# Each engine's order of steps, and each tile's buffer, from a written list instead of a planner

## The chip, the cores and the metric

The kernel runs on one core of one Trainium2 chip. The metric is the device time of one execution in microseconds (us). Engines are named as the profile names them: PE is TensorE, PEld its weight loads, DVE is VectorE, ACT is ScalarE, POOL is GpSimd, SP is SyncE.

## What is computed

Causal attention over a window of 96 keys plus 8 global ones, with a distance bias for each head, and then a two-layer MLP with h - tanh(h) between. All inputs and the output are float32.

```python
# q, k, v: (4, 8, 768, 64); w_in: (512, 2048); w_out: (2048, 512)
scores = q @ k.T / sqrt(64) + bias          # bias = -slope[head] * distance
keep = (key < 8) | ((0 <= row - key) & (row - key < 96))
a = softmax(where(keep, scores, -1e9))
x = (a @ v), heads side by side             # (3072, 512)
h = x @ w_in
out = (h - tanh(h)) @ w_out                 # (3072, 512)
```

## The kernel before, in words

The 3072 rows are cut into 24 **units** of 128 rows (4 batches of 6 blocks). The first block of every batch comes first, so units 0 to 3 need one block of keys, and the others two: their own (o=0) and the one before (o=1); a few columns of the batch's first block stand in for the global keys. A step has a name, a unit and perhaps a block, and one engine:

- `lk.u`, `lq.u`, `lv.u`: the loads of k, q and v, cast to bf16 on the way (L390, L393), on POOL's DMA queue; unit 0's k and q come as float32 on SP's and ACT's queues and are cast by `ck.0`, `cq.0`. `in.j`, `out.j` load parts of the weights (L396, L399), also on POOL.
- `rel`, `dist`, `slopes`, `first`, `turn`, `ident`, `ones`: constants, `rel` on POOL (L331), the others on DVE. `bm.m` (PE, L371) and `em.m` (ACT, L376) make three masks.
- `T.u` transposes q and k: on PE for units 0 to 6 (L408, L413, L417), with copies out of PSUM `Te.u.j` (ACT or DVE, L325, L327); from unit 7 on by a DMA on SP's queue (L425).
- `B.u` (units 0 to 2, L371) puts the bias into the scores' banks, `S.n` (L444) computes scores, `E.u.o` (ACT, L451) exponentiates, `M.u.o` (DVE, L455) multiplies the mask from unit 3 on, `AV.u` (PE, L470) multiplies with v, which has a column of ones for the sum, and `R.u` (DVE, L478, L479) divides. `K.u` and `V.u` (DVE) copy the global keys and values.
- `X.u` and `Xe.u` transpose the result: on PE (L490) and a copy for units 0 to 7, by a DMA on SP's queue (L501) from unit 8 on.
- The MLP goes by **groups**: units 0 and 1 alone, then two units each. `m1.g.f` (PE, L512) computes two of 16 column blocks of h (four for a single unit), `th.g.f` is tanh (ACT, L522), `g.g.f` subtracts (DVE, L528), `m2.u.c.a` (PE, L537) adds a quarter of the second product, `ev.u.c` copies the sum to SBUF (ACT or DVE, L325, L327) and `st.u.c` stores it (L546), on POOL for units 0 to 20 and on SP behind that.

All engines work through their own steps in order. The order is drawn up in Python while the program is built. `Plan` (from L17) holds every step with its engine, an estimated duration, its predecessors and what it takes and gives back: PSUM has 8 banks, and there are 5 buffers of `kq`, 12 of `vb`, 11 of `qk`, 5 of `pr`, 3 of `x`, 4 each of `xT`, `th`, `g` and `ot`. `Plan.run` (L59) walks through time and starts on every free engine the ready step with the best priority; loads and DMA transposes finish after an estimated time plus a slack. `AHEAD` and `T_AHEAD` (L557, L561) tie the scores and transposes to the progress of m1, `HOLD` (L560) keeps seven steps back. Where PE would stand still before 6.0 us of planned time, `warm` (L760) puts matmuls on a tile of zeros whose result nobody reads (lines 763 to 770). The buffers that the planner gave out are looked up by `buf`, `bank` and `banks` (L305 to L315). What a step waits for on the chip follows from the tiles that it reads and writes. SP's and POOL's DMAs take turns on 8 semaphores each, and a DMA waits for the one before it on its semaphore.

Of the kernel before, what the change touches and what calls it, by code (L numbers as in the profile page):

```python
# [16 lines left out]
class Plan:  # L17


    LAT = {PE: 0.21, ACT: 0.06, DVE: 0.06, POOL: 0.12, SP: 0.06}  # L20
    SLACK_DMA = 1.5
    SLACK_DT = 3.0
    SHARED = 2.5
    KEEP = 9
    BEHIND = (14.0, 23.5, 33.0)
    SLACK_ENG = 0.2
    EDGES = (20.0, 30.0, 180.0, 190.0)

    def __init__(self):
        self.ops, self.pools, self.paired, self.hold, self.cold = {}, {}, set(), {}, 0.0  # L30

    def pool(self, name, n, late=None):
        self.pools[name] = [0.0] * n
        for i, t in (late or {}).items():
            self.pools[name][i] = t

    def op(self, key, eng, us, fn, after=(), take=(), give=(), pri=0.0, ring=None, work=0.0, lag=0.0, tail=0.0,
           us2=None):
        self.ops[key] = dict(
            key=key, eng=eng if isinstance(eng, tuple) else (eng,), us=us, us2=us2, fn=fn,  # L40
            after=[a for a in after if a is not None], take=list(take), give=list(give), pri=pri, ring=ring,
            total={p: sum(m for _, x, m in take if x == p) for _, p, _ in take},
            work=work, lag=lag, tail=tail, n=len(self.ops),
        )

    def choose(self, p, n, have, now):
        have = sorted(g for g in have if g[0] <= now + 1e-9)
        if len(have) < n:
            return None
        if p not in self.paired:  # L50
            return sorted(i for _, i in have[:n])
        when = {i: t for t, i in have}
        both = sorted((max(when[i], when[i + 1]), i) for i in when if i % 2 == 0 and i + 1 in when)
        if n > 1:
            return sorted(i + j for _, i in both[: n // 2] for j in (0, 1)) if len(both) >= n // 2 else None
        lone = [g for g in have if g[1] ^ 1 not in when]
        return [(lone or have)[0][1]]

    def run(self, free):  # L59
        ops = self.ops  # L60
        need, users = {}, {}
        for key, o in ops.items():
            deps = set()
            for a in o["after"]:
                kind, k = ("issue", a[1]) if a[0] == "issue" else ("done", a)
                if k not in ops:
                    raise KeyError((key, a))
                deps.add((kind, k))
            need[key] = len(deps)
            for d in deps:  # L70
                users.setdefault(d, []).append(key)
        holds, left = {}, {}
        for key, o in ops.items():
            for g in o["give"]:
                left[g] = left.get(g, 0) + 1
        avail = {p: [(t, i) for i, t in enumerate(ts)] for p, ts in self.pools.items()}
        late = sorted({t for ts in self.pools.values() for t in ts if t > 0})
        events, tick = [], 0
        ready = {e: [] for e in (PE, ACT, DVE, POOL, SP)}
        busy = dict(free)  # L80
        order, start = [], {}
        rings, upto, version = {}, 0.0, 0

        def margin(t, most):
            a, b, c, d = self.EDGES
            return most * min(1.0, max(0.0, min((t - a) / (b - a), (d - t) / (d - c))))

        def push(t, what, key):
            nonlocal tick
            tick += 1  # L90
            heapq.heappush(events, (t, tick, what, key))

        def fits(o, now):
            left = {p: avail[p] for p in o["total"]}
            for h, p, n in o["take"]:
                ids = self.choose(p, n, left[p], now)
                if ids is None:
                    return False
                left[p] = [g for g in left[p] if g[1] not in ids]
            return True  # L100

        def drop(kind, key):
            for k in users.get((kind, key), ()):
                need[k] -= 1
                if need[k] == 0:
                    for e in ops[k]["eng"]:
                        ready[e].append(k)

        def flow(now):
            nonlocal upto  # L110
            live = [r for r in rings.values() if r]
            for r in live:
                r[0][1] -= (now - upto) / len(live)
            upto = now

        def again(now):
            nonlocal version
            version += 1
            live = [r for r in rings.values() if r]
            if live:  # L120
                push(now + max(0.0, min(r[0][1] for r in live)) * len(live), "flow", version)

        for e in busy:
            push(busy[e], "free", e)
        for t in late + sorted(self.hold.values()):
            push(t, "free", None)
        for key in ops:
            if need[key] == 0:
                for e in ops[key]["eng"]:
                    ready[e].append(key)  # L130
        while events:
            now, _, what, key = heapq.heappop(events)
            if what == "done":
                for g in ops[key]["give"]:
                    left[g] -= 1
                    if left[g] == 0:
                        h, part = g
                        p, ids = holds[h]
                        for i in ids if part is None else [ids[j] for j in part]:
                            avail[p].append((now, i))  # L140
                drop("done", key)
            elif what == "issued":
                drop("issue", key)
            elif what == "enter":
                flow(now)
                rings.setdefault(ops[key]["ring"], []).append([key, ops[key]["work"]])
                again(now)
            elif what == "flow":
                if key != version:
                    continue  # L150
                flow(now)
                for e, r in rings.items():
                    while r and r[0][1] <= 1e-9:
                        k, _ = r.pop(0)
                        more = margin(now, self.SLACK_DMA) + sum(1.0 for t in self.BEHIND if t < now < 40.0)
                        if k[0] in ("T", "Xe"):
                            shared = any(x for y, x in rings.items() if y is not e)
                            more = margin(now, self.SLACK_DT) + (self.SHARED if shared else 0.0)
                        push(now + ops[k]["tail"] + more, "done", k)
                again(now)  # L160
            if events and events[0][0] <= now + 1e-9:
                continue
            for e in (PE, ACT, DVE, POOL, SP):
                if busy[e] > now + 1e-9:
                    continue
                best, kept = None, False
                for k in sorted(ready[e], key=lambda x: (ops[x]["pri"], ops[x]["n"])):
                    o = ops[k]
                    if self.hold.get(k, 0.0) > now + 1e-9 or kept and "bank" in o["total"]:
                        continue  # L170
                    if fits(o, now):
                        best = ((o["pri"], o["n"]), k)
                        break
                    kept = kept or o["total"].get("bank", 0) >= self.KEEP
                if best is None:
                    continue
                k = best[1]
                o = ops[k]
                for x in o["eng"]:
                    ready[x].remove(k)  # L180
                for h, p, n in o["take"]:
                    ids = self.choose(p, n, avail[p], now)
                    avail[p] = [g for g in avail[p] if g[1] not in ids]
                    holds[h] = (p, ids)
                us = o["us"] if e is o["eng"][0] or o["us2"] is None else o["us2"]
                if e is PE and now < self.cold:
                    us *= 2.0
                end = now + us
                busy[e] = end
# [8 lines left out]
        if len(start) < len(ops):  # L198
            raise RuntimeError(f"no way on: {[k for k in ops if k not in start][:8]}")
# [617 lines left out]
```

## Time and profile before

| what | value |
|---|---|
| three executions | 215.68, 214.89, 214.81 us; median 214.89 us |
| span of the profiled execution, first to last instruction | 213.1 us |
| PE busy, DVE, ACT, POOL | 206.2, 130.8, 116.0, 79.8 us |
| m1 matmuls (L512), m2 matmuls (L537) | 90.2 and 85.7 us busy |
| first filler matmul, first mask matmul | 0.99, 3.10 us |
| first m1 matmul | 18.46 us |
| last PE instruction ends | 210.2 us |
| DMA of POOL's queue, DMA of SP's and ACT's queues | 18.88 MB and 7.61 MB |

The page gives the span of the profiled execution and not its own device time; the three executions lie 1.7 to 2.6 us over that span. Busy times of PE count overlapping matmuls with a modelled end, so two neighbouring steps can seem to overlap by some tenths of a us; distances between starts are exact. 19 of 400 records of L537 are missing from the trace.

### The profile page before, as it was taken

Reading aid. Unit: us, or ns where it says so; the run is one execution under the profiler, and the core shown is the slowest. Engines: PE = TensorE matmul, PEld = TensorE weight load, DVE = VectorE, ACT = ScalarE, POOL = GpSimd, SP = SyncE. Lnnn points to the kernel's source line nnn. Section 1 sums busy time; section 2 is a strip of 40 time slices with the busy share of each in tenths; the row PEclk is TensorE's granted clock in tenths of the full one; section 3 lists DMA queues with packets and bytes.
Section 4 is the critical chain, followed back from the end, with each engine's and each line's share of the span. In section 5 each row is a group of like instructions: output and inputs, shape, how many; then the busy total and the mean of one; then the engine's idle time right before and its main releaser. Section 6 shows DMA issues by size and latency. Waiting matters only on the chain.

```text
span 213.1 us, 5043 instructions
## 1 busy us (share of the span) xinstructions
PE 206.2 (97%) x2053; PEld 142.4 (67%) x2073; DVE 130.8 (61%) x267; ACT 116.0 (54%) x172; POOL 79.8 (37%) x105
## 2 busy tenths in 40 slices
PE   7998999999999999999999999999999999999994
PEld 2567876858656865965965955875855874968643
DVE  6469746727647972883872765891765795754600
ACT  4866535648455562864562753941935763545421
POOL 7995354659577404913603525401011100111000
PEclk9999999999999999999999999999999999999999
DMA  6999999999999993994993998987121411201012
GB/s 132 145 175 201 198 190 198 167 159 215 150 190 162 184 201 99 148 189 112 136 151 67 139 131 128 132 189 113 49 71 55 123 28 25 77 32 67 3 49 100
DMA packets 100886, 27.06 MB, mean 127 GB/s; under 512 B 91840, under 2 KB 99264, under 8 KB 100864
## 3 DMA queue, kind: packets, MB, share of 16 engines
q0 software_dynamic: 73088, 18.88, 92.3%
q1 hardware_dynamic: 27504, 7.61, 22.5%
q8 instruction: 16, 0.26, 0.5%
q10 hardware_dynamic: 272, 0.26, 0.5%
q14 instruction: 6, 0.05, 0.1%
HBM read 27.26 MB, written 6.29 MB: 157 GB/s over the span
## 4 chain that ended last, share of the span: by engine, by line
PE 91%; DVE 3%; DMA 3%; issue 1%; POOL 1%; ACT 0%; POOLq 0%; DVEq 0%
PE ps L512 39%; PE ps L537 39%; PE ps L470 5%; PE ps L444 5%; DMA kq<-in_q_dram 3%; PE ps L417 1%; DVE x L479 1%; PE ps L490 1%; DVE slopes L361 0%; PE ps L408 0%; POOL vb L393 0%; DVE qk L327 0%; POOL kq L390 0%; DVE rden L478 0%; DVE pr L455 0%
## 5 line engine op out<-in xcount | busy, mean ns | idle before, releaser
L512 PE MATMUL ps<-xT,w_in_bf 128*128 128x256 bf16 (+1 forms) x832 | 90.2, 264 | 0.0
L537 PE MATMUL ps<-w_out_bf,g 128*128 128x512 bf16 (+2 forms) x381 | 85.7, 370 | 1.2 <-issue 0.3
L512 PEld LDWEIGHTS <-w_in_bf 128*128 128x128 bf16 x832 | 74.5, 98 | 10.7
L522 ACT ACTIVATE th<-ps 128x512 f32<-128x512 f32 x96 | 56.0, 604 | 32.6 <-PE ps L512 29.3
L528 DVE TENSOR_TENSOR g<-ps,th 128x512 bf16<-128x512 f32 x96 | 62.5, 682 | 12.7 <-ACT th L522 11.8
L537 PEld LDWEIGHTS <-g 128*128 128x128 bf16 x400 | 37.4, 98 | 38.3
L451 ACT ACTIVATE pr<-ps 128x1024 bf16<-128x1024 f32 x44 | 42.5, 1023 | 20.5 <-PE ps L444 20.5
L546 POOL DMA_DIRECT2D out_dram<-ot x21 | 12.1, 574 | 95.1 <-ACT ot L325 71.0
L455 DVE TENSOR_TENSOR pr<-pr,mk 128x1024 bf16<-128x1024 bf16 x41 | 27.8, 688 | 10.9 <-ACT pr L451 10.7
L325 ACT COPY ot<-ps 128x512 f32<-128x512 f32 (+2 forms) x17 | 9.5, 560 | 33.8 <-PE ps L537 33.8
L393 POOL DMA_DIRECT2D vb<-in_v_dram x24 | 21.6, 900 | 6.2 <-DMA w_out_bf<-in_moe_w_out_dram 3.4
L393 POOL DMA_DIRECT2D kq<-in_q_dram x19 | 17.0, 897 | 5.7 <-PE ps L470 2.0
L393 POOL DMA_DIRECT2D kq<-in_k_dram x19 | 17.1, 899 | 3.5 <-DMA qk<-kq 1.6
L479 DVE TENSOR_TENSOR x<-ps,rden 128x512 bf16<-128x512 f32 x24 | 16.6, 692 | 0.8
L327 DVE COPY qk<-qk 128x32 bf16<-128x32 bf16 x16 | 3.6, 228 | 19.3 <-PE ps L444 19.3
L470 PEld LDWEIGHTS <-pr 128*128 128x128 bf16 x352 | 13.4, 97 | 2.8 <-ACT pr L451 0.4
L470 PE MATMUL ps<-vb,pr 128*128 128x65 bf16 x352 | 14.7, 193 | 0.4 <-ACT pr L451 0.2
L444 PEld LDWEIGHTS <-qk 64*128 64x128 bf16 x352 | 10.1, 94 | 7.1 <-issue 6.5
L478 DVE RECIPROCAL rden<-ps 128x8 f32<-128x8 f32 x24 | 5.0, 207 | 15.3 <-PE ps L470 14.9
L444 PE MATMUL ps<-qk 64*128 64x128 bf16 x192 | 9.5, 218 | 0.4 <-DVE rden L478 0.3
L444 PE MATMUL ps<-qk,qk 64*128 64x128 bf16 x160 | 7.8, 216 | 0.0
L327 DVE COPY ot<-ps 128x512 f32<-128x512 f32 x8 | 5.5, 692 | 3.0 <-PE ps L537 2.9
(43 smaller groups left out, 65.3 us busy)
## 6 DMA issues: line engine op xcount, KB each, us to landing
out_dram<-ot POOLq DMA_DIRECT2D x21, 256.0 KB, 3.9
vb<-in_v_dram POOLq DMA_DIRECT2D x24, 128.0 KB, 6.9
kq<-in_k_dram POOLq DMA_DIRECT2D x23, 128.0 KB, 5.9
kq<-in_q_dram POOLq DMA_DIRECT2D x23, 128.0 KB, 6.5
w_out_bf<-in_moe_w_out_dram POOLq DMA_DIRECT2D x4, 512.0 KB, 13.6
w_in_bf<-in_moe_w_in_dram POOLq DMA_DIRECT2D x3, 512.0 KB, 12.1
w_in_bf<-in_moe_w_in_dram POOLq DMA_DIRECT2D x2, 256.0 KB, 6.2
out_dram<-ot SPq DMA_DIRECT2D x2, 256.0 KB, 2.0
```

Of the source, the lines that this page charges most:

```text
L325: nc.scalar.copy(out=out, in_=in_)
L393: eng(e).dma_start(out=dst, in_=rows_of(src, u).rearrange("h p d -> p h d"))
L444: nc.tensor.matmul(bank(("s", u, o), hh)[:, p * P : (p + 1) * P], buf(("qk", back[u] if o else u))[r, 1, p, :], buf(("qk", u))[r, 0, p, :] ...
L451: nc.scalar.activation(d, banks(("s", u, o), 0, 1), AF.Exp, bias=0.0, scale=scale)
L455: nc.vector.tensor_tensor(out=t, in0=t, in1=mk[:, mask_of(u, o)], op=ALU.mult)
L470: nc.tensor.matmul(t[:, h // (H // 2), h % (H // 2), :], buf(("p", u, o))[:, slot(h), :], buf(("v", back[u] if o else u))[:, h, :], start= ...
L479: nc.vector.tensor_tensor(out=buf(("x", u)).rearrange("q (a h) d -> q a h d", a=2), in0=t[:, :, :, 0:Dh], in1=rden.to_broadcast([P, 2, H / ...
L512: nc.tensor.matmul(t[:, (f - f0) * n : (f - f0 + 1) * n], w_in_bf[j][:, c, fo : fo + P], x[:, c, 0:n], start=(c == 0), stop=(c == CD - 1),)
L522: nc.scalar.activation(h_view(buf(("th", g, f0)), g, m), h_view(bank(("h", g, f0)), g, m), AF.Tanh, bias=0.0, scale=1.0)
L528: nc.vector.tensor_tensor(out=buf(("g", g))[:, f0 : f0 + m, 0:n], in0=h_view(bank(("h", g, f0)), g, m), in1=h_view(buf(("th", g, f0)), g, ...
L537: nc.tensor.matmul(bank(part)[:, 0 : c1 - c0], buf(("g", g))[:, f, t * P : (t + 1) * P], w_out_bf[f // FJ][:, f % FJ, c0:c1], start=(f == ...
L546: eng(e).dma_start(out=out[turn_of[u] * P : (turn_of[u] + 1) * P, c0:c1], in_=buf(("ot", u))[:, c0:c1])
```

## The change

The planner is gone, with the durations, priorities and slacks that fed it. The source now holds two lists. `ORDER` names all 792 steps in one row; each engine works through its own in that order. Where a step can run on ACT or DVE, `/a` or `/d` says which. `HOMES` says which buffer or which PSUM banks a tile has. The functions that do the steps are the same, and so are the numbers of buffers. Three things differ in what runs. The word `warm` does not occur in `ORDER`, so there are no matmuls on zeros. 26 steps move between ACT and DVE; ACT has 177 steps (173 before) and DVE 218 (222). The order differs on every engine: PE's differs from its first step (`bm.0 B.0 bm.2 T.0 T.3` now, `bm.1 bm.2 bm.0 B.0 T.0` before), POOL's starts with `lq.3` ahead of `rel`, units 2 and 3 are loaded ahead of unit 1, v of units 0 and 1 is the last v ahead of the first weights, and the sums of several units (`m2`) are open at once.

```diff
-class Plan:
...
-    def run(self, free):
...
-        return order, start, {h: ids for h, (p, ids) in holds.items()}, now
+ORDER = """
+lq.0 lk.0 zero lq.3 ones.0 table rel lk.3 dist lq.2 slopes lk.2 first turn lk.1 bm.0 ident ones.1 lq.1 B.0 cq.0/a
+ck.0/d bm.2 lk.4 em.0 T.0 lv.3 em.2 T.3 lq.4 Te.0.0/d Te.0.1/a lv.2 B.2 Te.3.1/d Te.3.0/a T.2 lv.0 S.3 Te.2.1/a
+Te.2.0/d lv.1 E.3.0 S.2 T.1 in.1 E.2.0 M.3.0 in.0 S.0 Te.1.1/d AV.3 Te.1.0/a in.2 B.1 R.3 E.0.0 S.1 lv.4 AV.2 T.4 R.2
+E.1.0 out.0 AV.0 in.3 Te.4.0/d X.2 Te.4.1/a AV.1 Xe.2/d out.1 X.3 bm.1 R.1 Xe.3/a lq.5 em.1 R.0 S.4 lk.5 E.4.1 K.4 X.0
+X.1 Xe.0/d m1.2.2 Xe.1/d E.4.0 in.4 M.4.1 m1.2.0 th.2.2 M.4.0 m1.1.0 th.2.0 g.2.2 m1.0.0 th.1.0 g.2.0 lv.5 m1.2.4
+g.1.0 th.0.0 out.2 m1.0.4 g.0.0 th.2.4 g.2.4 m1.2.6 th.0.4 m1.1.4 g.0.4 th.2.6 out.3 g.2.6 AV.4 th.1.4 m2.1.0.0 R.4
+m2.2.0.0 V.4 g.1.4 m2.0.0.0 X.4 lq.7 m1.2.8 Xe.4/a m1.2.10 th.2.8 m1.0.8 g.2.8 th.2.10 lk.7 g.2.10 m1.1.8 th.0.8 lk.6
+g.0.8 m2.0.0.1 th.1.8 lq.6 T.5 g.1.8 m2.1.0.1 Te.5.1/a Te.5.0/d S.5 m2.2.0.1 E.5.0 K.5 lk.9 m1.2.12 E.5.1 M.5.0 lv.9
+m1.0.12 th.2.12 M.5.1 m1.1.12 th.0.12 g.2.12 AV.5 th.1.12 g.0.12 m2.3.0.0 V.5 R.5 m1.2.14 lq.9 g.1.12 X.5 th.2.14
+m2.0.0.2 Xe.5/d g.2.14 m1.3.10 lk.8 m1.3.2 th.3.10 lq.8 m1.3.6 g.3.10 th.3.2 lq.13 m1.3.8 g.3.2 T.7 th.3.6 m2.1.0.2
+g.3.6 lv.6 th.3.8 m2.2.0.2 g.3.8 T.9 T.6 m2.3.0.1 lk.10 Te.6.1/a Te.6.0/d m2.1.0.3 lv.7 T.8 S.6 ev.1.0/a m2.2.0.3
+E.6.1 K.6 m1.3.14 ev.2.0/d lq.11 E.6.0 m2.0.0.3 M.6.1 th.3.14 M.6.0 S.7 ev.0.0/a g.3.14 m1.3.4 E.7.1 K.7 m2.3.0.2
+lk.12 th.3.4 M.7.1 m1.3.0 E.7.0 g.3.4 lq.10 AV.6 th.3.0 lk.11 M.7.0 m1.3.12 R.6 lv.8 m2.3.0.3 th.3.12 g.3.0 lq.12 S.9
+ev.3.0/a V.6 m2.4.0.0 g.3.12 lk.14 E.9.1 K.9 AV.7 st.2.0 E.9.0 M.9.1 m2.4.0.1 V.7 m2.5.0.0 T.10 R.7 S.8 M.9.0 T.11 X.6
+E.8.0 m2.4.0.2 Xe.6/d X.7 E.8.1 M.8.0 m2.4.0.3 T.12 Xe.7/d AV.9 ev.4.0/a M.8.1 m2.5.0.1 V.9 R.9 AV.8 lk.15 m1.4.2 R.8
+Xe.9 lv.10 m1.4.14 th.4.2 Xe.8 lk.13 S.10 g.4.2 th.4.14 m1.4.4 lv.12 E.10.0 K.10 g.4.14 m1.4.6 lv.16 th.4.4 M.10.0
+m1.4.8 E.10.1 lk.17 g.4.4 m2.5.0.2 lv.11 th.4.6 M.10.1 m1.4.0 th.4.8 g.4.6 lq.17 g.4.8 S.11 th.4.0 lq.18 m2.5.0.3
+E.11.0 K.11 g.4.0 st.1.0 m1.5.8 E.11.1 M.11.0 m1.4.12 T.13 th.5.8 M.11.1 m1.5.2 th.4.12 g.5.8 m2.6.0.0 th.5.2 g.4.12
...
+g.12.14 m2.21.0.2 m2.20.0.3 m2.22.0.3 ev.20.0/a m2.21.0.3 st.20.0 ev.22.0/a m2.23.0.0 st.22.0 ev.21.0/a st.21.0
+m2.23.384.0 ev.23.0/a st.23.0 ev.23.384/a st.23.384
+"""
+HOMES = """
+mk.0:0,1 mk.1:0,1 mk.2:4,5 f32.0.k:1 kq.0:0 f32.0.q:0 kq.1:3 v.0:2 v.1:3 kq.2:2 kq.3:1 v.2:1 kq.4:4 v.3:0 v.4:4 kq.5:0
+v.5:5 kq.6:2 v.6:7 kq.7:1 v.7:8 kq.8:4 v.8:9 kq.9:3 v.9:6 kq.10:2 v.10:10 kq.11:1 v.11:5 kq.12:3 v.12:11 kq.13:0
+v.13:2 kq.14:4 v.14:7 kq.15:2 v.15:8 kq.16:1 v.16:4 kq.17:1 v.17:10 kq.18:3 v.18:5 kq.19:1 v.19:6 kq.20:0 v.20:3
...
-    def buffers(name, n, shape, dt, late=None):
+    def buffers(name, n, shape, dt):
         bufs[name] = [pool.tile(shape, dt, name=f"{name}{i}") for i in range(n)]
-        plan.pool(name, n, late)
-
-    plan = Plan()
-    WARM, COLD = (1.05, 6.0), 4.6
...
+    homes = {}
+    for word in HOMES.split():
+        name, ids = word.split(":")
+        homes[name] = [int(i) for i in ids.split(",")]
+
+    def home(holder):
+        return homes[".".join(map(str, holder))]
...
-    AHEAD = 5.5
...
-    T_AHEAD = 4.5
...
+    def op(key, eng, fn):
+        acts[".".join(map(str, key))] = (eng, fn)
...
-    order, start, got, end = plan.run(free)
-    holds.update(got)
...
     def warm():
         nc.tensor.matmul(ps[:, 7, :], zero[:, 0, :], zero.to_broadcast([P, 4, P]), start=True, stop=True)

-    pe = sorted((t, plan.ops[key]["us"]) for t, key, e in order if e is PE)
...
-        while last + 0.05 + (0.43 if last < COLD else 0.22) <= min(t, WARM[1]):
-            steps.append((last, -1, None, PE))
...
+    done = set()
     with tc.manual_schedule(engines={PE, ACT, DVE, POOL, SP}):
-        for t, n, key, e in sorted(steps, key=lambda s: s[:2]):
-            if key is None:
+        for word in ORDER.split():
+            if word == "warm":
                 warm()
-            else:
-                plan.ops[key]["fn"](e)
...
+                continue
+            name, _, side = word.partition("/")
+            e, fn = acts[name]
+            fn({"a": ACT, "d": DVE}[side] if e is None else e)
+            done.add(name)
+    assert done == set(acts), sorted(set(acts) - done)
```

## The prediction

> **What bounds the kernel now.** I read the page first (busy shares, the 40 slices, the chain that ended last), then the stages by window, then TensorE's instructions in order over the first 20 us.
>
> ```profile
> span 213.1 us, 5043 instructions
> PE 206.2 (97%) x2053; PEld 142.4 (67%) x2073; DVE 130.8 (61%) x267; ACT 116.0 (54%) x172; POOL 79.8 (37%) x105
> ...
> PE   7998999999999999999999999999999999999994
> ...
> PE 91%; DVE 3%; DMA 3%; issue 1%; POOL 1%; ACT 0%; POOLq 0%; DVEq 0%
> ```
>
> TensorE is busy in 97% of the span and carries 91% of the chain. The stages say where the rest is (columns: stretch, its length, PE busy with the number of matmuls, then the other engines):
>
> ```profile
> 1.00:6.50 5.50, 5.28 (x13) 1.64 (x14) 3.31 (x28) 3.60 (x4) 5.01 (x7) 1.00 0.98 160
> 6.50:10.00 3.50, 3.30 (x43) 2.18 (x41) 1.98 (x3) 2.70 (x5) 3.50 (x6) 1.00 1.44 137
> 10.00:15.00 5.00, 4.57 (x73) 3.18 (x74) 3.40 (x7) 3.30 (x5) 5.00 (x8) 1.00 1.63 180
> 15.00:20.00 5.00, 4.19 (x81) 3.37 (x76) 3.98 (x10) 4.14 (x6) 4.13 (x5) 1.00 1.46 188
> ```
>
> and, from the same view over 20 to 210.2 us, in ten stretches, their sum:
>
> ```profile
> sum 190.20, PE 188.83 PEld 132.05 DVE 117.92 ACT 101.98 POOL 61.81; mean PE 18.88 PEld 13.20 DVE 11.79 ACT 10.20 POOL 6.18
> ```
>
> That is 188.83 of 190.20 busy, 1.4 us missing. I compared the distance between the first matmuls of neighbouring steps with their matmuls' own time (0.1092 us for 256 columns, 0.2158 for 512). Changing between m1, m2 and AV costs nothing; a run of scores S costs 0.10 on the way in and 0.12 on the way out, whatever its neighbours. The one real wait is X.4, 0.32 us, for the division of unit 4 (the chain goes from AV to L478, L479 and L490 at 29.7 to 31.2). So after 20 us a better order has 0.3 us to win. The stage that can change is the start:
>
> ```profile
> 0.99 1.89 PE L761 MATMUL ps<-zero 128*128 128x512 bf16 x4 [0.99 <-DVE vb L367]
> 3.10 3.36 PE L371 MATMUL ps<-slopes,dist 128*128 128x512 bf16 x8 [0.22 <-DVE dist L338]
> ...
> 6.51 1.04 PE L413 MATMUL ps<-turn,kq 128*128 128x128 bf16 x8
> 7.48 1.06 PE L417 MATMUL ps<-turn,kq 128*64 128x128 bf16 x16
> ...
> 8.82 0.61 PE L371 MATMUL ps<-slopes,dist 128*128 128x512 bf16 x2
> ...
> 18.19 0.43 PE L470 MATMUL ps<-vb,pr 128*128 128x65 bf16 x8 [0.20 <-DVE pr L455]
> 18.46 1.05 PE L512 MATMUL ps<-xT,w_in_bf 128*128 128x128 bf16 x16
> 19.65 0.40 PE L490 MATMUL ps<-ident,x 128*128 128x128 bf16 x4
> 19.89 2.37 PE L512 MATMUL ps<-xT,w_in_bf 128*128 128x128 bf16 x28
> ```
>
> Here are the five filler matmuls on `zero`, the masks at 0.427 us a matmul (8 in 3.36) where the same line later takes 0.227 (2 apart by 0.227 at 8.82), and then transposes, scores and products held up by loads: AV.3 at 18.19 by v3, which landed at 17.82. From 19.89 TensorE never stops.
>
> **The change, part by part.** The reference line: at 19.89 the old order has done every TensorE step that the new list puts ahead of its first m1 (m1.2.2), and m1.0.0 besides (16 matmuls of 0.0558, 0.9 us). So m1.2.2 at 19.0 is break-even; each us beyond is a us lost, because nothing behind it can be made up but the 0.3.
>
> *Fillers out, constants later.* POOL now issues lq.3 ahead of `rel`. The first DMA on POOL took 1.03 us, so `rel` (0.34) runs at 1.87 instead of 0.84 and DVE's constants start at 2.25 instead of 1.22. DVE now does dist (1.01), slopes (0.82), first (0.41), and TensorE's first step, bm.0, needs all three: 2.25+1.01+0.82+0.41+0.05 = 4.54. Before, the first real matmul was at 3.10 (and the first filler at 0.99).
>
> *The clock.* In the trace matmuls went from 0.427 to 0.227 at 6.07, 5.1 us after the first filler. I give the new list the same 5.1 us from 4.54: full speed at 9.6. Then bm.0, B.0 and bm.2 are six matmuls at 0.427: to 7.10. How long T.0 and T.3 take at the low clock, no row shows: they take 0.109 a matmul (8 in T.0) at the high clock, twice the 0.055 of X with as many columns. Either the strided output sets the 0.109, and the low clock leaves it (0.9 + 1.0 us), or it doubles (1.7, and about 1.2 for T.3 until 9.6 has come). I take the first, as 0.109 is already what 128 columns cost at 0.427 per 512; the other end adds 1.0 and stays in the range.
>
> The page "TensorE: Matmul & The Clock Gate" of the Trainium skill (section on the HAM clock gate) says that the array's clock is halved until a window of about 3.4 us has been busy, and that the window runs freely, so the switch can come one to two windows after the start. By that rule the switch would come between 8.0 and 11.4 here; The trace agrees: 6.07 minus 0.99 is 5.1 us, between one window and two. It speaks against taking the fillers away.
>
> *The chain to m1.2.2*, with occupancies from the rows (T 1.0, S 0.33, AV 0.25, X 0.24, B 0.43, a reader starts 0.2 after the matmuls end): T.0 to 7.97, T.3 to 8.97, B.2 half slow to 9.7, T.2 to 10.7, S.3 to 11.03. S.2 waits for Te.2.0 (10.9+0.69): 11.6 to 11.95. T.1 to 12.95, S.0, AV.3 to 13.55, B.1 to 13.98, S.1, AV.2 to 14.55. T.4 writes the banks that AV.3 used, and R.3 (0.93) frees them at 14.7: to 15.7. AV.0, X.2, AV.1 to 16.45. Behind that VectorE is late: Te.4.0 and Xe.2 hold it to 17.0, then the list has R.1 ahead of R.0: 17.0 to 17.93 and 17.93 to 18.86. X.3, bm.1 and S.4 fit beside this (S.4's second block waits for R.1). X.0 waits for R.0: 18.9; X.1; **m1.2.2 at 19.4**, 0.4 past break-even. The loads don't hold this chain: POOL's ring landed its eleventh load at 14.81; v1 is now the twelfth, at about 15.5 (one more v at 0.95, an earlier start), and AV.1 wants it at 16.2. in.1 and in.0 (1.34 each in the old landings) follow by 18.3, wanted at 19.4 and 20.3.
>
> *The m1/m2 part.* X.4 now has three m2 steps (2.6 us) between it and AV.4, and its division takes 1.2 to 1.5: the 0.32 goes. Everything else can only add waits. Bank reuse has often 1.7 us between the matmuls that fill a bank and the next writer; the old order has the same (m1.11.14 behind g.11.8) without a wait. The tail (m2.23, ev, st; 210.2 to 213.1) is the same.
>
> Moved DMAs: units 9 to 17 now compute their scores 5 to 14 us earlier than before by counted TensorE work, in the stretch (40 to 80) where the DMA engines are full: transposes there took 6 to 9 us to land, loads 6 to 10. I walked POOL's and SP's queues. lk.10 waits for T.6 (47.7), lk.12 for T.9's landing (about 54, as kq.9 and kq.12 share a buffer), and behind it stand lq.10, lk.11, lv.8, lq.12, lk.14, st.2.0. lq.10 lands at about 59.5, T.10 8 us later at 67.6; S.10 stands 61.4 us of TensorE work into the list, with the start's 7.7 at 69.1. That clears by 1.5. st.2.0 lands at about 65, ev.4.0 needs its buffer at 65.7. Xe.8 (in the old run 6.9 us at this place) is wanted 8.1 us after AV.8 and takes 1.2+6.9 with its division. All three clear by 0 to 1.5 us: I cost them at nothing, and the cover is that margin.
>
> Sum: +0.4 at the start, -0.3 at X.4: **+0.1 us**. The page gives a span (213.1) and no time of its own for the profiled execution; against the median of 214.89 about 1.8 us lie around it. 214.89+0.1 = **215.0**.
>
> **The rivals.**
> *Cold start (slower side).* The T steps double at the low clock, or full speed comes a window later. Place: T.0, T.3, B.2. Price: 0.9 to 1.7 us, all of it on the chain above, since Te.2, S.2, T.1 hang on T.2; it decides from a T.3 end beyond 9.8 instead of 8.97. For: six masks at 0.427; against: 0.109 may be the output's own rate. The clock page named above allows the later switch. 215.0+1.3 = 216.3.
> *DMA late (slower side).* T.10, Xe.8 or st.2.0 lands later than its 0 to 1.5 us of margin, as loads and transposes asked for earlier share full engines. For: transposes up to 8.8 us in 45 to 67; against: those were issued at the same crowding as I assumed. It decides when a transpose takes over 9 us: TensorE stands 1 to 3 us at 69 or 76. 217.0.
> *Start wins.* If the clock is up by 8 and VectorE's chain is shorter than I add up, v1 bounds: AV.1 at 15.3, R.1, R.0 to 17.4, X.0, X.1, m1.2.2 at 17.9, 1.1 under break-even, with X.4's 0.3: 213.5.
> *The list is in effect the same order* (no change): TensorE's two lists differ from the first step, so no more than chance, and it falls within the forecast's band.
>
> **How the numbers follow.** Chances: forecast 0.52 (own range 214.4 to 215.9), cold start 0.20, DMA late 0.18, start wins 0.10. About 0.5% (1.07 us) is what a measurement of this kernel can tell from no change: bounds 213.8 and 216.0. Faster: most of the start's win, 0.09. Slower: most of cold start (216.0 to 216.7) and DMA late, 0.35. Same: 0.56. Range 213.8 to 217.4: it takes in the doubled T (216.0) and most of the DMA rival, and leaves out 0.2 at both ends.
>
> **What would show it.** First real matmul at 4.5 and the 0.427 to 0.227 switch near 9.6 (matmuls of L371); T.0's and T.3's spacing before it, 0.109 or 0.218; m1.2.2 (first L512) at 19.4 behind R.0; no gap at X.4; waits of PE on `qk<-kq`, `xT<-x` or ACT's ev near 65 to 76, absent in my forecast. Last matmul at 210.3. I am wrong if the first L512 is before 18.5 or after 20.5, or if TensorE waits over 1 us after it.

## The result and the profile after

The changed kernel takes 215.90 us (median of 5, 215.60 to 216.75); the kernel before, beside it, 214.81 us (median of 5, 214.53 to 215.68). The ratio is 1.0048, 95% interval 1.0028 to 1.0067: some 1.0 us slower, with an interval that lies on both sides of the 0.5% that the prediction took as its bound. The ratios here leave disturbed executions out and are not the quotients of the medians; they differ from them by up to 0.2%.

The profiled execution of the changed kernel took 215.62 us, the fastest but one of the five. Its page (span, busy time of the engines, TensorE in 40 slices, the chain by engine):

```profile
span 213.5 us, 5023 instructions
...
PE 202.8 (95%) x2040; PEld 141.9 (66%) x2068; DVE 130.6 (61%) x263; ACT 120.5 (56%) x176; POOL 79.3 (37%) x105
...
PE   0989999999999999999999999999999999999994
...
PE 93%; DVE 3%; issue 1%; POOL 1%; ACT 0%; POOLq 0%; DVEq 0%
```

TensorE was 97% busy and is 95%. Only the first slice differs visibly: 0 where 7 stood. The chain's 3% of waits for DMA are gone. The first stages by window, with the columns of before:

```profile
1.00:6.50 5.50, 1.51 (x4) 0.58 (x5) 3.17 (x28) 2.34 (x3) 5.14 (x8) 1.00 0.85 161
6.50:10.00 3.50, 3.50 (x28) 2.26 (x27) 1.11 (x2) 2.19 (x4) 3.50 (x5) 1.00 1.42 167
10.00:15.00 5.00, 4.39 (x77) 3.01 (x77) 2.88 (x6) 4.31 (x6) 5.00 (x8) 1.00 1.98 159
15.00:20.00 5.00, 4.47 (x80) 3.45 (x79) 4.16 (x11) 4.08 (x7) 3.87 (x5) 1.00 1.42 195
```

From 6.5 to 10 TensorE is busy all the time and yet does 28 matmuls where it did 43: it is slow, not idle. Its timeline (start, length, line, count, idle before it) shows why:

```profile
4.99 2.74 PE L277 MATMUL ps<-slopes,dist 128*128 128x512 bf16 x6 [4.99 <-DVE dist L251]
7.52 1.33 PE L319 MATMUL ps<-turn,kq 128*128 128x128 bf16 x8
8.78 1.06 PE L323 MATMUL ps<-turn,kq 128*64 128x128 bf16 x16
...
12.16 0.40 PE L350 MATMUL ps<-qk 64*128 64x128 bf16 x8 [0.46 <-DVE qk L233]
...
19.18 0.62 PE L396 MATMUL ps<-ident,x 128*128 128x128 bf16 x8 [0.45 <-DVE x L385]
19.63 4.57 PE L418 MATMUL ps<-xT,w_in_bf 128*128 128x256 bf16 x56
```

Six masks at 0.427, then T.0: the starts of its eight matmuls are 0.213 apart up to 8.11 and 0.109 apart behind it. That is the clock switch: the trace's own clock record starts its entry at full clock at 8.11 too. S.2 waits for Te.2.0, X.0 waits for R.0, and the first m1 starts at 19.63 (18.46 before). Behind it the trace has one wait, 0.14 us ahead of m1.5.8, and none at X.4. (The three waits at L443 put down to "issue", 0.5 us, stand at lost records.)

**The account.** The distance from the first m1's start to the last matmul's is 191.56 us before. 0.32 of it is X.4. Without any wait the new list has 190.65 (e1, e6 and e7 below agree to the hundredth), so another 0.59 lies behind the first m1 in the old order alone: 0.53 of it is X.3 with the wait ahead of it (from 19.35, where m1.0.0 is done, to 19.89), which the new list has ahead of its first m1; 0.06 is not traced to a step. So break-even for the first m1 is 18.46 + 0.59 = 19.05. The changed kernel: +0.58 at the start, -0.32 at X.4, +0.14 at m1.5.8, in sum +0.40; the last matmul starts at 210.43 instead of 210.02, and the span grows by 0.4.

### The profile page after: what moved, and what is told of

It is laid out like the page before. It is cut to its first block, busy times and chain, and to the rows that moved or that the text cites. A ratio compares the mean times of both kernels' runs of the same rounds, so it can differ in the third digit from the quotient of the medians.

```text
span 213.5 us, 5023 instructions
## 1 busy us (share of the span) xinstructions
PE 202.8 (95%) x2040; PEld 141.9 (66%) x2068; DVE 130.6 (61%) x263; ACT 120.5 (56%) x176; POOL 79.3 (37%) x105
## 3 DMA queue, kind: packets, MB, share of 16 engines
HBM read 27.26 MB, written 6.29 MB: 157 GB/s over the span
## 4 chain that ended last, share of the span: by engine, by line
PE 93%; DVE 3%; issue 1%; POOL 1%; ACT 0%; POOLq 0%; DVEq 0%
PE ps L418 40%; PE ps L443 39%; PE ps L350 5%; PE ps L376 5%; PE ps L277 2%; PE ps L323 1%; DVE x L385 1%; PE ps L396 1%; DVE qk L233 1%; PE ps L319 1%; DVE slopes L267 0%; PE ps L314 0%; POOL kq L296 0%; DVE rden L384 0%; DVE far L243 0%
## 5 line engine op out<-in xcount | busy, mean ns | idle before, releaser
L418 PE MATMUL ps<-xT,w_in_bf 128*128 128x256 bf16 (+1 forms) x832 | 91.9, 264 | 0.0
L443 PE MATMUL ps<-w_out_bf,g 128*128 128x512 bf16 (+2 forms) x373 | 88.4, 370 | 1.7 <-issue 0.5
L434 DVE TENSOR_TENSOR g<-ps,th 128x512 bf16<-128x512 f32 x96 | 65.7, 688 | 35.0 <-ACT th L428 33.6
L428 ACT ACTIVATE th<-ps 128x512 f32<-128x512 f32 x96 | 57.1, 597 | 49.3 <-PE ps L418 48.7
L443 PEld LDWEIGHTS <-g 128*128 128x128 bf16 x400 | 36.7, 98 | 33.2
L357 ACT ACTIVATE pr<-ps 128x1024 bf16<-128x1024 f32 x44 | 43.1, 1022 | 11.1 <-PE ps L350 10.4
L231 ACT COPY ot<-ps 128x512 f32<-128x512 f32 (+2 forms) x22 | 12.4, 565 | 18.7 <-PE ps L443 18.7
L277 PE MATMUL ps<-slopes,dist 128*128 128x512 bf16 x11 | 4.3, 516 | 5.0 <-DVE dist L251 5.0
```

Source lines behind the costliest of these rows:

```text
L231: nc.scalar.copy(out=out, in_=in_)
L357: nc.scalar.activation(d, banks(("s", u, o), 0, 1), AF.Exp, bias=0.0, scale=scale)
L418: nc.tensor.matmul(t[:, (f - f0) * n : (f - f0 + 1) * n], w_in_bf[j][:, c, fo : fo + P], x[:, c, 0:n], start=(c == 0), stop=(c == CD - 1),)
L428: nc.scalar.activation(h_view(buf(("th", g, f0)), g, m), h_view(bank(("h", g, f0)), g, m), AF.Tanh, bias=0.0, scale=1.0)
L434: nc.vector.tensor_tensor(out=buf(("g", g))[:, f0 : f0 + m, 0:n], in0=h_view(bank(("h", g, f0)), g, m), in1=h_view(buf(("th", g, f0)), g, ...
L443: nc.tensor.matmul(bank(part)[:, 0 : c1 - c0], buf(("g", g))[:, f, t * P : (t + 1) * P], w_out_bf[f // FJ][:, f % FJ, c0:c1], start=(f == ...
```

## The experiments

The theories. **Clock** (A in the expectations): with the fillers gone, TensorE's clock goes up later, and the matmuls from the first mask to the switch cost double. **Constants** (B): what hurts is that `rel` stands behind lq.3 on POOL, so that the masks start at 5.0 instead of 3.1. **Transpose** (D, formed after the first four runs from what held of C, which put the loss behind the start): m1.5.8 stands right where Xe.8's DMA may or may not have landed, so an execution can lose up to 1 us there. Rival to all: the list itself is the worse order, so that undoing these leaves 1.005.

Every experiment's kernel ran 12 times, with 35 or 23 executions of the kernel before on the same chip; the first two rows are the five executions each of the result. e1 to e4 ran on one chip, e5 to e8 on a second, e9 and e10 on a third, so between these groups only ratios can be compared. The columns behind the ratio are from one profiled execution each: the time of the switch (where the spacing changes and the trace's clock record starts at full clock), the first m1, first m1 to last matmul, and what the latter holds over its least. The profile's own idle time is up to 0.2 shorter than these waits, as it counts from a modelled end. A profiled execution need not be a typical one: e1's and e10's are the fastest of their twelve, e8's is the slowest, and e2's is 0.7 above its median.

| run | median | ratio [95%] | switch | first m1 | first m1 to last | waits in it |
|---|---|---|---|---|---|---|
| before | 214.81 | | 6.08 | 18.46 | 191.56 | X.4 0.32 |
| changed | 215.90 | 1.0048 [1.0028, 1.0067] | 8.11 | 19.63 | 190.79 | Xe.8 0.14 |
| e1_fill | 215.07 | 1.0010 [0.9990, 1.0030] | 4.22 | 18.40 | 190.65 | none |
| e2_rel | 215.09 | 0.9997 [0.9977, 1.0017] | 7.00 | 19.21 | 191.40 | Xe.8 0.75 |
| e3_fill_rel | 215.35 | 0.9999 [0.9981, 1.0016] | 4.69 | 18.71 | 191.40 | Xe.8 0.75 |
| e4_old_nofill | 215.66 | 1.0009 [0.9987, 1.0030] | 7.04 | 18.92 | 191.55 | X.4 |
| e5_new_again | 216.14 | 1.0048 [1.0029, 1.0066] | 7.64 | 19.40 | 191.54 | Xe.8 0.89 |
| e6_swap | 215.72 | 1.0016 [1.0003, 1.0030] | 9.31 | 20.21 | 190.65 | none |
| e7_fill_swap | 215.16 | 0.9990 [0.9965, 1.0014] | 4.33 | 19.45 | 190.65 | none |
| e8_fill_swap_early | 214.88 | 0.9971 [0.9944, 0.9997] | 4.86 | 17.90 | 192.32 | Xe.11 1.23 |
| e9_xe11 | 214.75 | 0.9977 [0.9956, 0.9998] | 4.46 | 17.83 | 191.09 | none |
| e10_early_again | 215.32 | 1.0000 [0.9977, 1.0024] | 3.93 | 18.19 | 191.09 | none |

(e8 to e10 do X.0 and X.1 behind the first m1, so their least is 191.09. The edits below show parts of long lines of `ORDER`.)

### e1_fill: fillers back in the new list

```diff
-lq.0 lk.0 zero lq.3 ones.0 table rel lk.3 dist
+lq.0 lk.0 zero lq.3 ones.0 warm warm warm warm warm warm warm warm warm table rel lk.3 dist
```

> The new list with nine filler matmuls on zeros put at its start (0.99 to about 4.8 us, where TensorE stood still); nothing else differs. Theory A (the clock): without work before 4.99 us the new list runs its masks, T.0 and part of T.3 at the low clock (a T matmul took 0.213 us there, 0.109 after), and how much of them depends on when in a free-running rhythm the switch falls: 8.11 us in the profile, later in the executions of 216.7. With fillers the switch comes by about 6.1, T.0 runs at 0.109, its start moves from 7.52 to about 6.8, the first m1 from 19.63 to about 18.9, and the executions lie within 0.5 us: median 214.9 (214.6 to 215.2). Theory B (late constants: rel stands behind lq.3 on POOL): the first mask stays at 4.99, the fillers change nothing that counts: 215.6 to 215.9. Theory C (late DMAs after 40 us make the slow executions): 215.0 at the fastest, but executions 1 us above still occur.

TensorE's start in e1_fill:

```profile
0.99 3.69 PE L539 MATMUL ps<-zero 128*128 128x512 bf16 x9 [0.99 <-DVE vb L273]
4.98 1.47 PE L277 MATMUL ps<-slopes,dist 128*128 128x512 bf16 x6 [0.30 <-DVE dist L251]
6.29 1.04 PE L319 MATMUL ps<-turn,kq 128*128 128x128 bf16 x8
```

The first mask starts when it did (4.98), but six now take 1.47 instead of 2.74, and T.0 stands at 6.29 instead of 7.52. The first m1 comes 1.23 us earlier, and the ratio falls from 1.0048 to 1.0010. So with the clock up, the late constants cost nothing that the times show. The traced execution, at 214.29 the fastest of the twelve, has more of the gain than the median (215.07). And the times lie within 2.6 us where theory A expected 0.5, so the switch isn't all that varies.

### e2_rel, e3_fill_rel: `rel` ahead of lq.3, without and with fillers

```diff
-lq.0 lk.0 zero lq.3 ones.0 table rel lk.3 dist
+lq.0 lk.0 zero rel lq.3 ones.0 table lk.3 dist
```

(e3_fill_rel has six `warm` behind `ones.0` too.)

> The new list with rel ahead of lq.3 on POOL, no fillers; nothing else differs. Theory A (the clock): the first mask moves from 4.99 to about 3.7, but the work at the low clock stays, and the switch still falls where its rhythm has it; T.0 starts at about 6.3 at the half rate and the first m1 comes 0.3 to 0.8 us earlier; executions still spread by about 1 us: median 215.3 (214.9 to 215.9). Theory B (late constants): the whole 1.2 us comes back, first m1 at 18.4, median 214.7 and little spread.

> The new list with rel ahead of lq.3 and six fillers from 0.99 us to the first mask at about 3.7. Theory A: the switch comes by about 6.1 and the masks begin 1.2 us earlier, T.0 at about 6.2 at full rate; then the v loads bound the chain (v1 landed at 15.39): first m1 at 18.0 to 18.5, median 214.3 (214.0 to 214.7), spread within 0.5. Theory B: the same as with rel alone, 214.7.

The masks start at 3.71 in both. e2 is as fast as e1 (0.9997): an earlier first matmul brings the switch forward as well, to 7.00. If late constants had a price of their own, e3 would have to win over e1 what e1 left. It doesn't (0.9999), and its timeline says what is in the way:

```profile
3.71 1.93 PE L277 MATMUL ps<-slopes,dist 128*128 128x512 bf16 x6
5.48 1.04 PE L319 MATMUL ps<-turn,kq 128*128 128x128 bf16 x8
7.26 1.06 PE L323 MATMUL ps<-turn,kq 128*64 128x128 bf16 x16 [0.75 <-DMA kq<-in_k_dram]
```

T.0 stands 0.81 earlier than in e1, and T.3 waits 0.75 for unit 3's k. The two cures don't add: e3 was expected at 214.0 to 214.7 with its first m1 at 18.0 to 18.5, and has 215.35 and 18.71; with the clock up, the loads are the bound. It holds the other way round as well: with `rel` early, the fillers add nothing that the times show (0.9997 without, 0.9999 with them). So neither theory stands alone. Late constants and the low clock lengthen the same stretch, and either cure takes that back.

Nor does e2 get all of it in its trace:

```profile
15.43 0.42 PE L376 MATMUL ps<-vb,pr 128*128 128x65 bf16 x8 [0.26 <-DMA vb<-in_v_dram]
...
16.40 0.42 PE L376 MATMUL ps<-vb,pr 128*128 128x65 bf16 x8 [0.33 <-DMA vb<-in_v_dram]
```

T.4 stands 1.20 earlier than in the changed kernel's first trace (14.11 for 15.31), but behind the waits for v of units 0 and 1 only 0.40 is left (16.40 for 16.80). An execution in which these land earlier would keep more. Whether this is why e2's median is 0.8 us under the changed kernel's, though its trace also waits 0.75 at m1.5.8, stays open.

### e4_old_nofill: the kernel before without its fillers

```diff
         while last + 0.05 + (0.43 if last < COLD else 0.22) <= min(t, WARM[1]):
-            steps.append((last, -1, None, PE))
```

> The old kernel without its five fillers, the planned order unchanged. Theory A: TensorE's first work is at 3.10 us, the switch comes at 6.5 to 9.9 instead of 6.07, T.0 and T.1 run in part at the half rate; but the old chain waits for q2 until 11.27 anyway, so most of it is hidden where the switch comes before 11: 214.8 to 215.4, and a spread larger than the old kernel's. If the fillers are worth nothing: 214.8.

```profile
3.10 3.60 PE L371 MATMUL ps<-slopes,dist 128*128 128x512 bf16 x8 [3.10 <-DVE dist L338]
6.49 1.31 PE L413 MATMUL ps<-turn,kq 128*128 128x128 bf16 x8
7.73 1.06 PE L417 MATMUL ps<-turn,kq 128*64 128x128 bf16 x16
...
10.62 1.06 PE L417 MATMUL ps<-turn,kq 128*64 128x128 bf16 x16
...
17.44 0.40 PE L490 MATMUL ps<-ident,x 128*128 128x128 bf16 x4 [0.16 <-DVE x L479]
18.66 0.42 PE L470 MATMUL ps<-vb,pr 128*128 128x65 bf16 x8 [0.83 <-DMA vb<-in_v_dram]
```

The switch moves from 6.08 to 7.04, and the second transpose starts 0.25 later (7.73 for 7.48). The third starts where it did, at 10.62 for 10.61, as the kernel before waits there for a load:

```profile
10.61 1.32 PE L417 MATMUL ps<-turn,kq 128*64 128x128 bf16 x16 [0.17 <-DMA kq<-in_k_dram]
...
17.59 0.40 PE L490 MATMUL ps<-ident,x 128*128 128x128 bf16 x4 [0.16 <-DVE x L479]
```

So the low clock's cost is hidden by then, as theory A had it for this kernel, and the transpose ahead of AV.3 comes even 0.15 earlier. The first m1 does come 0.46 later (18.92 for 18.46), but that is AV.3's wait for v of unit 3, which was issued at the same time as before (11.07 for 11.10) and landed at 18.62 instead of 17.82: another execution's load, and not shown to come from the fillers. The times don't settle what the fillers are worth in the old order: the medians lie 0.57 us apart, the ratio says 0.2, and its interval is -0.3 to +0.6 us.

### e5_new_again, e6_swap, e7_fill_swap: m1.5.8 moved

e5_new_again is the changed kernel unchanged. In e6_swap two ready steps stand ahead of m1.5.8; e7_fill_swap has the fillers too.

```diff
-m1.5.8 E.11.1 M.11.0 m1.4.12 T.13 th.5.8 M.11.1 m1.5.2 th.4.12 g.5.8 m2.6.0.0 th.5.2 g.4.12 AV.10 g.5.2
+m1.4.12 E.11.1 M.11.0 m2.6.0.0 T.13 th.4.12 M.11.1 m1.5.8 g.4.12 m1.5.2 th.5.8 g.5.8 th.5.2 AV.10 g.5.2
```

> The new list unchanged, beside the three below on one chip: how far its executions lie apart, and a second trace of it. Theory A (the clock: nothing on TensorE before 4.99 us, so the switch to full speed falls anywhere between about 7 and 11.5): median 215.7 (215.4 to 216.1), executions from 215.0 to 217; in this trace the switch lies elsewhere than at 8.11 and the first m1 moves with it. Theory D (the DMA transpose Xe.8 lands late for m1.5.8, by 0.16 us in the first trace of the new list and 0.76 in two of its variants): the wait before m1.5.8 differs from the first trace by some tenths.

> The new list with m1.4.12 and m2.6.0.0 put ahead of m1.5.8 (1.73 us more between AV.8 and m1.5.8), no fillers. Theory D: the wait for xT<-x goes, and with it 0.2 to 0.8 us: median 0.4 below the new list unchanged, and a smaller spread. Theory A: less than 0.3 below, the spread stays.

> Nine fillers and the move of m1.5.8 together. If both theories hold, the gains add: 0.8 from the clock and 0.2 to 0.6 from the wait, median 214.5 (214.2 to 214.9). If A alone holds: 215.0, as with the fillers alone. No wait of TensorE over 0.2 us behind the first m1.

The same place in the changed kernel's first trace, and in e5_new_again's, which is the same program:

```profile
75.15 1.04 PE L443 MATMUL ps<-w_out_bf,g 128*128 128x512 bf16 x4
76.17 2.78 PE L418 MATMUL ps<-xT,w_in_bf 128*128 128x256 bf16 x24
```

```profile
74.92 1.04 PE L443 MATMUL ps<-w_out_bf,g 128*128 128x512 bf16 x4
76.69 2.78 PE L418 MATMUL ps<-xT,w_in_bf 128*128 128x256 bf16 x24 [0.73 <-DMA xT<-x]
```

Behind four m2 matmuls an m1 that waits for nothing comes 0.88 after the first of them, as e6_swap shows below. m1.5.8 comes 1.02 after it in one execution (0.14 late) and 1.77 in the other (0.89 late). Xe.8's transpose landed at 76.03 in the first and at 76.55 in the other, 7.64 us after its issue, and in both m1.5.8 starts 0.14 behind the landing. In e6_swap the same place has m1.4.12, and no wait follows:

```profile
75.72 1.04 PE L443 MATMUL ps<-w_out_bf,g 128*128 128x512 bf16 x4
76.60 1.04 PE L418 MATMUL ps<-xT,w_in_bf 128*128 128x256 bf16 x8
77.47 1.03 PE L443 MATMUL ps<-w_out_bf,g 128*128 128x512 bf16 x4
```

Xe.8 landed at 76.72 in e6 and at 76.20 in e7, where m1.4.12 starts at 76.60 and 75.83: in its old place m1.5.8 would have waited 0.26 and 0.51. The ratio falls from 1.0048 to 1.0016, though this profiled execution had the latest switch of all (9.31). e6's 12 times lie within 0.8 us of each other instead of 2.1; but e7's, with the same move, lie within 2.7, so the smaller spread is not shown to be the move's. With both cures (e7) the ratio is 0.9990. Each alone takes 0.3 to 0.4%, both 0.6%, as two separate losses would, and the traces have them at two places. The times alone don't show that they add: e7's interval holds e1's 1.0010, and its median of 215.16 misses the 214.2 to 214.9 expected of both. e7's own trace shows a third thing that varies, a load (v of unit 1, landed at 16.59):

```profile
16.63 0.42 PE L376 MATMUL ps<-vb,pr 128*128 128x65 bf16 x8 [1.19 <-DMA vb<-in_v_dram]
```

### e8_fill_swap_early, e9_xe11, e10_early_again: the first m1 ahead of X.0 and X.1

e8 is e7 with m1.2.2 right behind S.4, so that units 2 and 3 fill the wait for R.0. For that Xe.2 goes to ACT and four tiles get other banks. e9 moves one more m1 behind two ready m2 steps; e10 is e8 once more, beside e9.

```diff
-R.0 S.4 lk.5 E.4.1 K.4 X.0 X.1 Xe.0/d m1.2.2 Xe.1/d
+R.0 S.4 m1.2.2 lk.5 E.4.1 K.4 X.0 X.1 Xe.0/d Xe.1/d
```

```diff
-ev.6.0/a V.12 m1.6.8 R.12 th.5.12 T.15 m2.7.0.0 g.5.12 th.6.8 m2.9.0.2 g.6.8
+ev.6.0/a V.12 R.12 th.5.12 T.15 m2.9.0.2 m2.7.0.0 g.5.12 m1.6.8 th.6.8 g.6.8
```

> As the kernel with fillers and the move of m1.5.8, and besides m1.2.2 ahead of X.0 and X.1 (its group does not need them), in bank 0 instead of bank 2, which AV.0 holds until R.0 is done; Xe.2 on ScalarE. If the division R.0 is what the first m1 waits for at 18.4, m1.2.2 starts at about 17.8, when em.1 has freed bank 0, and 0.4 to 0.6 us are won: median 214.0 (213.6 to 214.4). If the w_in loads bound the start instead (in.1 landed at 17.4, in.0 at 18.75), the gain shrinks to 0.1 to 0.3.

> The kernel of e8_fill_swap_early with one more move: m2.9.0.2 and m2.7.0.0 (two m2 steps of units 9 and 7, whose operands are long there) now stand ahead of m1.6.8, the first m1 that reads the transposes of units 10 and 11; in e8 that step waited 1.06 us for a transpose's DMA, though e7 with the same order at this place had no wait there. Theory D (a transpose's landing varies by a microsecond and more between executions, and an m1 right behind it pays): the wait at this place goes, TensorE has no wait over 0.3 us behind its first m1, last minus first m1 falls from 192.3 to 191.2 (190.65 as in e1, e6 and e7, and X.0 and X.1 that now lie behind the first m1), and the times gather: median 214.4 to 214.8, ratio 0.996. Rival (that wait was one odd execution): the median and spread are those of e8, ratio 0.997. Rival (the new place is worse, as the m2 step now waits for a store's buffer on ACT): a wait of some tenths at L443, ratio 0.998 or more.

> The kernel of e8_fill_swap_early unchanged, on the same chip as e9_xe11 and against the kernel before once more: ratio 0.995 to 0.999 if the gain is of the kernel and not of that chip and hour. Theory D: with or without a wait for a transpose behind the first m1, by the execution. Theory A (the clock): the first m1 between 17.6 and 18.2, as the fillers bring the switch to 4.2 to 5.

e8's first m1 stands at 17.90, 1.15 under break-even, of which 0.44 are X.0 and X.1 that now come behind it. Its trace gives the rest back at one line, the first m1 of units 10 and 11:

```profile
92.27 1.03 PE L418 MATMUL ps<-xT,w_in_bf 128*128 128x256 bf16 x8
94.36 1.05 PE L418 MATMUL ps<-xT,w_in_bf 128*128 128x256 bf16 x8 [1.06 <-DMA xT<-x]
```

e10, the same program, has no wait there: what was seen at m1.5.8 is back at the next pair of units, in some executions. In e9 the two m2 steps stand in that place and the m1 follows without a wait. That is no proof of the move: Xe.11 landed at 90.72 in this execution (94.32 in e8), so the m1 would not have waited in its old place, at 93.07, either.

```profile
92.20 1.03 PE L418 MATMUL ps<-xT,w_in_bf 128*128 128x256 bf16 x8
93.28 1.67 PE L443 MATMUL ps<-w_out_bf,g 128*128 128x512 bf16 x7
94.80 1.04 PE L418 MATMUL ps<-xT,w_in_bf 128*128 128x256 bf16 x8
```

On one chip e9 has 214.75 and e10 215.32. e8's median of 214.88 lies above the 213.6 to 214.4 expected, and its gain (0.9971) was not found again in e10 (1.0000), so only e9's stands, and barely: 0.9977, interval 0.9956 to 0.9998 against the kernel before. Against the changed kernel it is about 0.7% (0.9977 over 1.0048, from two chips).

## Why the prediction was right, and where it was not

The time was 215.90 for 215.0, in the stretch called "same" (within 0.5%), but by a hair, and at the upper end of the forecast's own range. The places named were the right ones; several terms were not.

1. **Reference line, m1.2.2 at 19.0.** Right: 19.05 by the account.
2. **First matmul at 4.54.** It was 4.99. The step that failed is `rel` at 1.87: POOL's first DMA began at 1.27 and not at 0.84, so `rel` ran at 2.20, which is 0.33 of the 0.45.
3. **Switch 5.1 us after the first matmul, at 9.6.** Wrong in size: 3.1 us here, and 2.6, 4.3, 3.3 and 3.9 in e5, e6, e2 and e4. One distance from one trace was taken for a constant, and it is a draw. In the three traces of the new list with neither fillers nor `rel` moved, the first m1 follows it on a straight line: 7.64, 8.11 and 9.31 give 19.40, 19.63 and 20.21, 0.49 us for each us of switch. Half is what a stretch at half clock must cost.
4. **T.0 and T.3 at 0.109 at the low clock.** Wrong: 0.213, doubled, which is the first half of the rival called cold start. In e6, with the switch at 9.31, the whole of T.0 is slow:

```profile
4.99 2.74 PE L277 MATMUL ps<-slopes,dist 128*128 128x512 bf16 x6 [4.99 <-DVE dist L251]
7.52 1.92 PE L319 MATMUL ps<-turn,kq 128*128 128x128 bf16 x8
9.37 0.41 PE L323 MATMUL ps<-turn,kq 128*64 128x128 bf16 x4
```

Errors 3 and 4 cancel in the changed kernel's trace: an earlier switch than assumed, over transposes that suffer more. In e6 they don't: its first m1 is 1.16 past break-even (20.21 less 19.05), 0.76 more than the forecast's 0.4, where the rival was priced at 1.3 more.

The page "TensorE: Matmul & The Clock Gate" of the Trainium skill (section on the HAM clock gate) describes a free-running window of about 3.4 us, so that the switch's distance varies by the execution. The traces agree that it varies, but 2.6 us (e5) is less than one window; the measurement decides. That sentence in the prediction spoke against taking the fillers away, and e1 bears it out.

The traces show the rhythm themselves. Their clock records have the full clock last 208.21 us in ten executions and 204.80 us in two; the two differ by 3.413 us and are 61 and 60 times that. So in these traces the clock changes only at the ends of stretches of 3.413 us, whose place in an execution is a draw. A stretch need not be full of work: in e5 the one before the switch (4.23 to 7.64) held matmuls from 5.00 on, for 2.64 us, and that was enough. In the kernel before, fillers filled the last 1.7 us of the stretch that ended at 2.67, and the switch came only with the next end, 6.08.

5. **The chain to m1.2.2 at 19.4, behind R.0.** Right in kind and nearly in size: 19.63, and TensorE's last wait ahead of it is X.0 for the division. T.2 ended 0.6 later than forecast; of that 0.35 was left where VectorE began R.1 (17.35 for 17.0) and 0.28 at X.0 (19.18 for 18.9).
6. **X.4's 0.32 goes.** Right.
7. **Three DMAs with 0 to 1.5 us of margin, costed at nothing.** T.10 and st.2.0 right. Xe.8 wrong: its margin was given as 0 to 1.5, and it was -0.14 and -0.89 in two executions of the same program. The step that failed is the term itself: a margin smaller than the spread of a landing has a price in the mean. The rival called DMA late named the place and the resource, and was too high in size (1 to 3 us).

Sum for the profiled execution: +0.40 (+0.58, -0.32, +0.14), where +0.1 was forecast. In e5's, whose time (216.12) is that of its median, it is +0.35 - 0.32 + 0.89 = +0.92, and the two medians of that chip differ by 0.94 (216.14 and 215.20). By e1 and e6, about half of the loss is the start, with constants late while the clock is low, and half is one transpose; that e2 alone took back all of it doesn't fit these halves and stays open. The order itself is not shown to be worse: free of both (e7), it is at 0.9990 (0.9965 to 1.0014).

## What to carry to other kernels

Where a start is short of work, matmuls on zeros can have a price and a gain to be worked out: what they buy is at most half of the time between the first real matmul and the clock's switch, and only if nothing else, such as a load, holds the work up by then (in e1's trace they gained 1.2 us; in e4's, without them, the work stood at the same load as before). A step placed right at the landing of a DMA costs on the average even if the one trace at hand shows next to no wait; two ready steps in between cost nothing that e6 shows. And a single trace is one draw: two traces of the same program differed by 0.75 us at one step here.

## What the runs showed of the hardware

- The switch of the masks' and fillers' matmuls from 0.427 us to the shorter spacing came 2.6 to 5.1 us after the first matmul in twelve traces. The granted clock in the rows by window reads 1.00 ahead of the switch as well (1.00 to 6.50 above), so those rows don't show it; the spacing does, and the trace's clock record, whose first entry at full clock starts at the same times.
- The full clock lasted 208.21 us in ten traces and 204.80 in two, 61 and 60 times 3.413 us; 2.64 us of work in one such stretch were enough for the switch (e5), 1.7 were not (before).
- The transposes on TensorE whose matmuls are 0.109 apart, twice the 0.055 of others with as many columns, still double at the low clock, to 0.213.
- DMA transposes of one shape (x to xT) took from 2.3 to 10.6 us to land within one execution (e8_fill_swap_early), and m1.5.8's wait for one of them varied from 0.14 to 0.89 us between two executions of the same program.
